# An expert's first product run by pairs of quarters: one change to a tuned attention and mixture-of-experts kernel

## The chip, the cores and the metric

The kernel runs on one core of one Trainium2 chip. The metric is device time in microseconds, the median of several executions: 2615.45 us for the kernel before (three runs, 2614.93 to 2617.84). One further execution was recorded by the hardware profiler; it took 2614.48 us, and its span from the first to the last instruction is 2612.6 us. All rows below are from that execution.

## The reference, cut to what matters

Three stages run one after the other on 3072 tokens of width 512, all in float32.

```python
x = chunked_attention(q, k, v, mem_k, mem_v)          # 4 x 8 heads, 768 tokens, head width 64
h = x @ w_in; x = (h * clip(h + 3, 0, 6) / 6) @ w_out # hidden width 2048
P = exp(x @ w_gate - max)                             # 3072 x 8
for _ in range(8): P = rows and columns of P normalised in turn (sinkhorn)
for e in range(8):
    h = maximum(x @ w1[e], 0)                         # 512 -> 1024
    out += P[:, e:e+1] * (h @ w2[e])                  # 1024 -> 512
```

## The kernel before, in words

Every large product is made of three TensorE passes on operands that are split into a high and a low part (`passes`, L192 to L196): high weight by high operand, high by low, low by high. ACT makes the high part (a copy with rounding, `split`, L178), DVE the low part (a subtraction, L183).

The first stage (attention) and the second (the dense layer) run together in a loop over `steps`: two passes over the hidden width, each over 8 tiles of 384 tokens and 8 slices f of the hidden width. One such f-step of pass two is 12 matmuls of the first kind and 12 of the second. The x tile of 384 tokens is spilled to DRAM in pass one and loaded again for pass two (`x_load`, L364; `x_split`, L368, one quarter kt at a time). Beside this a "factory" (L456) on GpSimd forms the sums of quarters of the expert weights w1 and w2 that the third stage needs and stores them in DRAM.

The third stage (L892 on) handles 3 token blocks of 1024 tokens; each block meets 8 experts, so there are NM = 24 pairs n of block and expert. Each product of an expert is done by a scheme with seven products in place of eight: weights and operands are seen as 2 x 2 quarters, seven combinations of weight quarters (A11, A12, A22 and the sums S1 to S4) meet seven operands (B11, B21, B22 and the sums T1 to T4). For the first product the operands of x (tiles `xo`) stay in SBUF for a whole token block; they are made by `x_ops` for the first block and half by half by `x_half_load` and `x_half` at the change of block. `FIRST` gives the order of the seven; k runs over four column tiles of the hidden half. `first_product(n, k, p)` is 2 x 3 = 6 matmuls of 512 columns into a PSUM tile. The terms of a quarter of h accumulate partly in PSUM: `first_out` copies partial sums into tiles `cp` (ACT, L648) for p 0 to 2, and for p 3 to 5 DVE adds a copy and the PSUM tile into a tile `g` (L657); for p 6 ACT applies relu directly (L655). In the next step `positive` applies relu in place (ACT, L663) and `gated` multiplies by the gate (GpSimd, L670). The weights w1 of one k come as one tile of 7 x 256 columns (`w1_load`, 384 KB and 512 KB), its high part is made by ACT (L567); its low part is made by DVE for the first token block (L576) and stored, and loaded from DRAM for the later blocks.

The second product takes h's tiles as operands: `make` forms the T sums of h in four parts (DVE L692, for the last expert half of it on GpSimd), the high parts `oh` (ACT L701) and low parts `ol` (DVE L706), and the high and low part of the w2 tile (L607, L613; the staging tile has one buffer, so the next load waits for it). `second_product(n, mi, q)` is again 6 matmuls; `second_out` adds its result to y (DVE L735).

What sets the order is written out by hand. `order` (L916) is a list of steps; a step holds a first product, a second product, or both. Each engine and SyncE's DMA queue run their instructions in the order in which this loop issues them, and wait in order. Before, 28 + LEAD = 33 first products come alone, then 5 second products alone, then pairs, and at the end 28 second products alone. `makes` puts the four parts of a second operand four steps ahead of its use. The sinkhorn iterations run as a generator between the steps (L947), on DVE, with small matmuls on TensorE; then `gates` writes the gates to DRAM and they are loaded, broadcast. `halves` (L936 to L940) puts the 14 halves of the next block's x operands into the steps after (n = last expert, k = 3, p = 0).

Of the kernel before, what the change touches and what calls it, by code (L numbers as in the profile page):

```python
# [1 line left out]

# [6 lines left out]
F32 = mybir.dt.float32  # L9
# [20 lines left out]
HB = 512  # L30
# [3 lines left out]
NG = 12  # L34
LEAD = 5
# [3 lines left out]
def attn_moe_moe(ctx: ExitStack, tc: tile.TileContext, qk, vw, wi, wo, wa, wb, wg, out):  # L39
# [41 lines left out]
    ws1 = [dr_p.tile([128, 2, 4, 256], F32, name=f"ws1{j}") for j in range(NP // 2)]  # L81
    ws2 = [dr_p.tile([128, 4, 4, 256], F32, name=f"ws2{e}") for e in range(NE)]
    wl1 = [dr_p.tile([128, 7, 256], F32, name=f"wl1{q}") for q in range(NP)]
# [309 lines left out]
    def sinkhorn():  # L393
# [12 lines left out]
        for _ in range(8):  # L406
# [36 lines left out]
    FIRST = ((A11, "B11", "a"), (S1, "T1", "c"), (S2, "T2", "a"), (A12, "B21", "b"), (S3, "T3", "a"),  # L443
             (S4, "B22", "c"), (A22, "T4", "a"))

# [5 lines left out]
            "T4": ("T2", "B21", "T2")}  # L451
    NM = NSB * NE
    xo = {}
    w1s, w1, w2s, w2, gq, op, yc = {}, {}, {}, {}, {}, {}, {}

    def factory():  # L456
# [8 lines left out]
        def of_w1(q):  # L465
# [11 lines left out]
            def store():  # L477
                nc.sync.dma_start(out=ws1[q // 2][:, q % 2], in_=t[1])
# [23 lines left out]
    def x_ops(sb, p, tag):  # L502
# [7 lines left out]
        for n in ("B11", "T1", "T2", "B21", "T3", "B22", "T4"):  # L510
# [30 lines left out]
    X_ORDER = ("B11", "T1", "T2", "B21", "T3", "B22", "T4")  # L541
# [15 lines left out]
    def w1_load(j):  # L557
        if j < NM * NF // 2:
            s = w1s[j] = w1s_p.tile([128, 7, 256], F32, tag="w1s", name="w1s")
            q = j % NP  # L560
            nc.sync.dma_start(out=s[:, :3], in_=wa[q].rearrange("p (a f) -> p a f", a=4)[:, 1:])
            nc.sync.dma_start(out=s[:, 3:], in_=ws1[q // 2][:, q % 2])

    def w1_hi(j):
        if j < NM * NF // 2:
            hi = w1_p_tile("h")
            nc.scalar.activation(out=hi, in_=w1s[j], func=AF.Copy)  # L567
            w1[j] = hi

    def w1_p_tile(t):  # L570
        return w1r_p.tile([128, 7, 256], F32R, tag=f"w1{t}", name=f"w1{t}", bufs=2)

    def w1_lo(j):
        if j < NP:
            lo = w1_p_tile("l")
            nc.vector.tensor_tensor(out=lo, in0=w1s.pop(j), in1=w1[j].bitcast(F32), op=ALU.subtract)  # L576
            w1[j] = w1[j], lo
        elif j < NM * NF // 2:
            w1[j] = w1[j], w1l.pop(j)

    def w1_lo_load(j):

        if NP <= j < NM * NF // 2:
            lo = w1l[j] = w1_p_tile("l")
            nc.sync.dma_start(out=lo.bitcast(F32), in_=wl1[j % NP])

    def w1_lo_store(j):
        if j < NP:
            nc.sync.dma_start(out=wl1[j], in_=w1[j][1].bitcast(F32))
# [460 lines left out]
```

## Time and profile before

| | |
|---|---|
| median of runs | 2615.45 us |
| profiled execution | 2614.48 us, span 2612.6 us, mean granted TensorE clock 0.988 |
| TensorE, VectorE, ScalarE, GpSimd busy | 98%, 69%, 53%, 38% |
| DMA | 543 MB, 208 GB/s mean |
| chain that ended last | TensorE 86%, VectorE 7%, DMA 3%, ScalarE 2% |

How to read it: PE is TensorE, PEld its weight loads, DVE is VectorE, ACT is ScalarE, POOL is GpSimd, SP is SyncE, whose queue issues the DMAs. In rows of instructions "out<-in" are the program's tile names and "x" a count; L is a line of the kernel. A wait row says who waited for whom: total us, times, longest. PEclk is the granted clock as a share of full speed.

### The profile page before, as it was taken

The page shows a single profiled execution, that of the slowest core. Times are in us where ns is not written, and L with a number is a line of the kernel's source. Part 1 is how long each engine was busy: PE and PEld are TensorE (multiplying, and loading weights), DVE is VectorE, ACT ScalarE, POOL GpSimd, SP SyncE. Part 2 cuts the span into 40 slices and gives each one's busy share as a digit, 9 for nine tenths or more (in the row PEclk, how much of TensorE's full clock was granted, in tenths as well). Part 3 has the DMA queues.
Part 4 walks back from the last instruction along what each step waited for, and adds up shares of the span by engine and source line. Part 5 has one row for each costly group of instructions (what it writes and reads, how often), then busy time and mean ns, then how long its engine had stood idle before and what let it go on. Part 6 is the DMA issues. An engine that isn't in the chain of part 4 may idle for free.

```text
span 2612.6 us, 34019 instructions
## 1 busy us (share of the span) xinstructions
PE 2550.9 (98%) x12621; PEld 2196.5 (84%) x12621; DVE 1812.7 (69%) x2115; ACT 1390.7 (53%) x2323; POOL 989.4 (38%) x693
## 2 busy tenths in 40 slices
PE   7999999999989999999989999999999999999998
PEld 7899999999968888888768888888878888888886
DVE  6767766557478999898875666666575566566666
ACT  6656654122255555555556555555565655555553
POOL 1035554454006535444432434433333334333332
PEclk9899999999999999999989999999999999999999
DMA  7468867775255666656656666665575655565643
GB/s 203 125 206 274 280 219 273 234 251 189 87 178 191 238 212 205 239 194 210 218 197 222 224 227 228 215 219 203 182 260 188 221 204 203 181 203 204 203 167 137
DMA packets 198102, 543.06 MB, mean 208 GB/s; under 512 B 18960, under 2 KB 80592, under 8 KB 197936
## 3 DMA queue, kind: packets, MB, share of 16 engines
q1 hardware_dynamic: 197936, 540.89, 61.4%
q8 instruction: 99, 1.62, 0.3%
q14 instruction: 67, 0.55, 0.1%
HBM read 414.89 MB, written 125.93 MB: 207 GB/s over the span
## 4 chain that ended last, share of the span: by engine, by line
PE 86%; DVE 7%; DMA 3%; ACT 2%; issue 1%; SPq 0%; POOL 0%; DVEq 0%; ACTq 0%
PE oa L195 6%; PE oa L196 6%; PE oa L194 6%; PE ga L195 6%; PE ga L196 6%; PE ga L194 6%; PE pa L194 3%; PE oc L195 3%; PE oc L196 3%; PE oc L194 3%; PE ph L194 3%; PE ph L195 3%; PE ph L196 3%; PE pa L196 3%; PE gc L194 3%; PE pa L195 3%
## 5 line engine op out<-in xcount | busy, mean ns | idle before, releaser
L670 POOL TENSOR_TENSOR g<-g,pb 128x512 f32<-128x512 f32 x368 | 676.7, 1855 | 1207.6 <-ACT g L663 1065.1
L701 ACT ACTIVATE oh<-g 128x1024 fp32r<-128x1024 f32 x336 | 355.3, 1058 | 540.2 <-PE oa L196 204.6
L706 DVE TENSOR_TENSOR ol<-g,oh 128x1024 fp32r<-128x1024 f32 x336 | 461.7, 1378 | 219.1 <-ACT oh L701 218.7
L692 DVE TENSOR_TENSOR g<-g 128x1024 f32<-128x1024 f32 x188 | 323.4, 1752 | 21.4 <-POOL g L670 21.4
L194 PE MATMUL ga<-xo,w1h 128*128 128x512 f32 x768 | 302.4, 394 | 9.0 <-DVE g L657 8.2
L195 PE MATMUL ga<-xo,w1h 128*128 128x512 f32 x768 | 300.7, 392 | 1.6 <-DVE xo L183 1.6
L195 PE MATMUL oa<-ol,w2h 128*128 128x512 f32 x768 | 300.1, 391 | 1.8 <-DVE ol L706 1.8
L194 PE MATMUL oa<-oh,w2h 128*128 128x512 f32 x768 | 300.4, 391 | 0.6 <-ACT oh L701 0.6
L196 PE MATMUL ga<-xo,w1l 128*128 128x512 f32 x768 | 300.2, 391 | 0.0
L196 PE MATMUL oa<-oh,w2l 128*128 128x512 f32 x768 | 299.9, 390 | 0.0
L607 ACT ACTIVATE w2h<-w2s 128x1024 fp32r<-128x1024 f32 x168 | 177.6, 1057 | 77.5 <-DMA w2s<-ws 29.5
L663 ACT ACTIVATE g<-g 128x512 f32<-128x512 f32 x288 | 174.9, 620 | 65.8 <-DVE g L657 65.7
L308 ACT ACTIVATE t<-ph,half 128x384 f32<-128x384 f32 x128 | 74.6, 582 | 223.6 <-PE ph L196 223.6
L463 POOL TENSOR_TENSOR fs<-fr 128x256 f32<-128x256 f32 x128 | 113.1, 883 | 205.5 <-DMA ws<-fs 196.9
L735 DVE TENSOR_TENSOR y<-y,oa 128x512 f32<-128x512 f32 x174 | 118.9, 683 | 97.9 <-PE oa L196 97.2
L194 PE MATMUL ph<-xh,wah 128*128 128x384 f32 x512 | 181.2, 354 | 1.0 <-ACT xh L178 1.0
L194 PEld LDWEIGHTS ga<-xo,w1h 128*128 128x128 f32 x768 | 145.1, 189 | 41.5 <-issue 5.5
L195 PE MATMUL ph<-xl,wah 128*128 128x384 f32 x512 | 175.7, 343 | 3.7 <-DVE xl L183 3.6
L196 PE MATMUL ph<-xh,wal 128*128 128x384 f32 x512 | 174.9, 342 | 0.0
L194 PE MATMUL pa<-hh,wbh 128*128 128x384 f32 x512 | 174.6, 341 | 0.0
L195 PEld LDWEIGHTS oa<-ol,w2h 128*128 128x128 f32 x768 | 144.9, 189 | 32.7 <-DVE ol L706 2.5
L195 PEld LDWEIGHTS ga<-xo,w1h 128*128 128x128 f32 x768 | 144.7, 188 | 32.6 <-DVE xo L183 3.5
(144 smaller groups left out, 5629.6 us busy)
## 6 DMA issues: line engine op xcount, KB each, us to landing
w1l<-wl SPq DMA_DIRECT2D x64, 896.0 KB, 7.2
w2l<-wl SPq DMA_DIRECT2D x112, 512.0 KB, 3.7
w1s<-ws SPq DMA_DIRECT2D x96, 512.0 KB, 4.8
w2s<-ws SPq DMA_DIRECT2D x96, 512.0 KB, 5.2
w1s<-in_wa_dram SPq DMA_DIRECT2D x96, 384.0 KB, 3.7
w2s<-in_wb_dram SPq DMA_DIRECT2D x144, 256.0 KB, 4.3
ws<-fs SPq DMA_DIRECT2D x64, 512.0 KB, 5.8
wl<-w1l SPq DMA_DIRECT2D x32, 896.0 KB, 7.4
```

The costliest lines, as they stand in the source:

```text
L194: nc.tensor.matmul(ps, wh, xh, start=start, stop=False, skip_group_check=more)
L195: nc.tensor.matmul(ps, wh, xl, start=False, stop=False, skip_group_check=more)
L196: nc.tensor.matmul(ps, wl, xh, start=False, stop=stop, skip_group_check=more)
L308: nc.scalar.activation(out=t, in_=ps, func=AF.Relu, scale=1.0 / 6.0, bias=half)
L463: nc.gpsimd.tensor_tensor(out=s[o], in0=a, in1=b, op=f)
L607: nc.scalar.activation(out=hi, in_=w2s[m], func=AF.Copy)
L663: nc.scalar.activation(out=g, in_=g, func=AF.Relu)
L670: nc.gpsimd.tensor_tensor(out=g, in0=g, in1=p, op=ALU.mult)
L692: eng.tensor_tensor(out=o, in0=gq[n, x, i], in1=gq[n, y, i], op=ALU.subtract)
L701: nc.scalar.activation(out=hi, in_=gq[n, b, i], func=AF.Copy)
L706: nc.vector.tensor_tensor(out=lo, in0=gq[n, b, i], in1=op[m, i].bitcast(F32), op=ALU.subtract)
L735: nc.vector.tensor_tensor(out=t, in0=t, in1=yo[c, dc], op=ALU.add)
```

## The change: what it does

The four k of a first product are taken in two pairs: for each pair and each p, both k in turn. A12 by B21 comes first, then A11 by B11; the partial sums are copied into the tiles of h themselves and completed there, so the tiles `cp` go, and h's tiles number 13 instead of 12. Per p and pair of k there is one small w1 tile of 2 x 256 columns, staged in three buffers and kept in seven; load, high part, low part and store are issued piece by piece, about six pieces ahead. The factory's w1 sums are laid out in DRAM to match. LEAD falls from 5 to 1, and no second products run alone before the pairs: 29 first products alone, then pairs, then 29 second products alone. The x operands are made in the new order, one half in each of 14 steps at a block change. The sinkhorn generator is advanced in two of three steps instead of four of seven, and the gates follow in it after a further yield. In pass one's last tile `x_load(0)` is issued at f = 1 instead of 3, and its four splits at f = 3 to 6 instead of 4 to 7.

```diff
-NG = 12
-LEAD = 5
+NG = 13
+LEAD = 1
-    ws1 = [dr_p.tile([128, 2, 4, 256], ...
+    ws1 = [dr_p.tile([128, 4, 2, 256], ...
-    wl1 = [dr_p.tile([128, 7, 256], F32, name=f"wl1{q}") for q in range(NP)]
+    wl1 = [dr_p.tile([128, 2, 256], F32, name=f"wl1{g}") for g in range(7 * NP // 2)]
-    FIRST = ((A11, "B11", "a"), (S1, "T1", "c"), (S2, "T2", "a"), (A12, "B21", "b"), (S3, "T3", "a"),
+    FIRST = ((A12, "B21", "b"), (A11, "B11", "a"), (S1, "T1", "c"), (S2, "T2", "a"), (S3, "T3", "a"),
              (S4, "B22", "c"), (A22, "T4", "a"))
+    FIRST_OUT = ("B11", "B11", "B22", "B12", "B22", "B12", "B21")
-        for n in ("B11", "T1", "T2", "B21", "T3", "B22", "T4"):
+        for n in X_ORDER:          # ("B21", "B11", "T1", "T2", "T3", "B22", "T4")
...
+    def w1_load(g):
+        if g < NW:
+            q, a = g // 7 % (NP // 2), FIRST[g % 7][0]
+            s = w1s[g] = w1s_p.tile([128, 2, 256], F32, tag="w1s", name="w1s", bufs=3)
+            if a < S1:
+                of = wa[2 * q:2 * q + 2].rearrange("k p (a f) -> p k a f", a=4)[:, :, a + 1]
+            else:
+                of = ws1[q][:, a - S1]
+            nc.sync.dma_start(out=s, in_=of)
+    def w1_hi(g):
+        if g < NW:
+            w1[g] = w1_p_tile("h")
+            nc.scalar.activation(out=w1[g], in_=w1s[g], func=AF.Copy)
+    def w1_lo(g):
+        if g < 7 * NP // 2:
+            lo = w1_p_tile("l")
+            nc.vector.tensor_tensor(out=lo, in0=w1s.pop(g), in1=w1[g].bitcast(F32), op=ALU.subtract)
...
     def first_product(n, k, p):
-        new = p in (0, 1, 3)
+        new = p < 3
-        wh, wl = w1[4 * n + k]
+        wh, wl = w1[7 * (2 * n + k // 2) + p]
...
     def first_out(n, k, p):
+        ps, b, i = ch[FIRST[p][2], k], FIRST_OUT[p], k // 2
+        if k % 2 == 0 and p in (0, 2, 3, 6):
+            gq[n, b, i] = g_p.tile([128, 2, HB], F32, tag="g", name="g", bufs=NG)
+        g = gq[n, b, i][:, k % 2]
+        if p in (0, 2, 3):
+            nc.scalar.activation(out=g, in_=ps, func=AF.Copy)
+        elif p == 6:
+            nc.scalar.activation(out=g, in_=ps, func=AF.Relu)
         else:
-            nc.vector.tensor_tensor(out=g, in0=cp[other], in1=ch[c], op=ALU.add)
+            nc.vector.tensor_tensor(out=g, in0=g, in1=ps, op=ALU.add)
...
-            if (pe, b) == (1, NB1 - 1):
-                for do, j in {2: ((w1_hi, 0),), 3: ((w1_lo, 0), (w1_load, 1)), 6: ((w1_hi, 1),),
-                              7: ((w1_lo, 1), (w1_load, 2))}.get(f, ()):
-                    do(j)
+            if (pe, b) == (1, NB1 - 1) and 1 <= f < 7:
+                w1_hi(f - 1)
+                w1_lo(f - 1)
+                if f < 6:
+                    w1_load(f + 2)
...
-                if f == 3:
+                if f == 1:
                     x_load(0)
...
-            if f >= 4 and n < NB1 and (pe or b == NB1 - 1):
-                x_split(n, f - 4)
+            r = f - (4 if pe else 3)
+            if 0 <= r < KT and n < NB1 and (pe or b == NB1 - 1):
+                x_split(n, r)
...
-        H = [(n, k, p) for n in range(NM) for k in range(4) for p in range(7)]
+        work = chain(sinkhorn(), gates())       # gates yields once after its copy
+        H = [(n, k + j, p) for n in range(NM) for k in (0, 2) for p in range(7) for j in range(2)]
-        order = [(H.pop(0), None) for _ in range(28 + LEAD)] + [(None, O.pop(0)) for _ in range(LEAD)]
+        order = [(H.pop(0), None) for _ in range(28 + LEAD)]
-        quarters = {3: "B11", 4: "B22", 5: "B12", 6: "B21"}
+        quarters = {1: "B11", 4: "B22", 5: "B12", 6: "B21"}
-                halves[base + 1 + r * 11 // 13] = halves.get(base + 1 + r * 11 // 13, []) + [(sb, r)]
+                halves[base + 1 + r] = [(sb, r)]
-            if work and i % 7 in (0, 1, 2, 6) and next(work, 0) == 0:
+            if work and i % 3 != 1 and next(work, 0) == 0:
...
+                g = 7 * (2 * n + k // 2) + p
+                if k % 2:
+                    w1_load(g + 8)
+                    w1_lo_load(g + 6)
+                    w1_hi(g + 6)
+                else:
+                    if g:
+                        w1_lo(g + 5)
+                    for m in range(4 if g == 0 else 0):
+                        w1_lo_store(m)
+                    w1_lo_store(g + 4)
```

## Rows read from the trace of the kernel before

**Rows 1.** The page's busy times: TensorE, us, share of the span, instructions.

```profile
PE 2550.9 (98%) x12621; PEld 2196.5 (84%) x12621; DVE 1812.7 (69%) x2115; ACT 1390.7 (53%) x2323; POOL 989.4 (38%) x693
```

**Rows 2.** Busy us (instructions) of each engine in eight stretches, clock, DMA share.

```profile
core 0: us, PE busy (x) PEld busy (x) DVE busy (x) ACT busy (x) POOL busy (x), PEclk, DMA share, GB/s
718.00:772.00 54.00, 49.95 (x224) 39.51 (x224) 39.08 (x96) 27.59 (x42) 0.00 (x0) 1.00 0.43 153
772.00:792.00 20.00, 14.77 (x59) 11.56 (x58) 15.20 (x13) 8.94 (x12) 3.37 (x2) 0.91 0.79 252
860.00:1240.00 380.00, 379.51 (x1673) 313.71 (x1672) 346.93 (x296) 211.40 (x264) 180.15 (x87) 1.00 0.64 216
1300.00:1365.00 65.00, 54.57 (x214) 42.38 (x213) 48.77 (x51) 35.55 (x48) 19.48 (x12) 0.89 0.54 184
1950.00:2015.00 65.00, 61.12 (x256) 48.90 (x255) 40.32 (x42) 34.45 (x44) 20.71 (x12) 0.95 0.55 195
2560.00:2580.00 20.00, 16.15 (x60) 11.99 (x60) 15.90 (x11) 7.44 (x8) 13.51 (x6) 0.91 0.42 139
430.00:440.00 10.00, 6.80 (x31) 6.23 (x30) 7.57 (x10) 3.71 (x7) 7.09 (x8) 0.83 0.77 258
440.00:450.00 10.00, 10.00 (x60) 10.00 (x59) 6.08 (x9) 4.61 (x9) 3.78 (x5) 1.00 0.83 281
```

**Rows 3.** TensorE's waits from 1280 to 1345 us: total us, times, longest.

```profile
PE ga L194 <- DVE g L657: 5.4, 2, 3.5
PE gc L194 <- ACT xo L178: 3.3, 1, 3.3
```

**Rows 4.** ScalarE's wait for loads of x halves, same stretch.

```profile
ACT xo L178 <- DMA xs<-x2d: 8.2, 2, 5.0
```

**Rows 5.** TensorE's longest wait from 760 to 860 us.

```profile
PE oc L194 <- ACT oh L701: 3.7, 1, 3.7
```

**Rows 6.** ScalarE's wait for the load of w2, 755 to 870 us.

```profile
ACT w2h L607 <- DMA w2s<-ws: 10.9, 3, 5.2
```

**Rows 7.** TensorE's waits from 380 to 450 us.

```profile
PE ph L195 <- DVE xl L183: 2.2, 1, 2.2
PE ph L194 <- ACT xh L178: 1.0, 1, 1.0
```

**Rows 8.** Timeline at the end: start us, duration us, engine, line, instruction.

```profile
2560.89 2.39 POOL L692 TENSOR_TENSOR g<-g 128x1024 f32<-128x1024 f32 x1
```

**Rows 9.** VectorE groups by line, 720 to 772 us: busy us, mean ns, idle before.

```profile
L576 DVE TENSOR_TENSOR w1l<-w1s,w1h 128x1792 fp32r<-128x1792 f32 x3 | 6.1, 2020 | 0.0
L657 DVE TENSOR_TENSOR g<-cp,gb 128x512 f32<-128x512 f32 x5 | 3.4, 686 | 0.5 <-PE gb L196 0.4
```

**Rows 10.** Groups of the x operands' halves, whole span.

```profile
L183 DVE TENSOR_TENSOR xo<-xs,xo 128x512 fp32r<-128x512 f32 x28 | 23.6, 852 | 18.1 <-ACT xo L178 18.1
L178 ACT ACTIVATE xo<-xs 128x512 fp32r<-128x512 f32 x28 | 17.2, 622 | 16.2 <-DMA xs<-x2d 11.2 <-DMA xs<-xt 5.0
```

**Rows 11.** Timeline of pass one's end: a subtraction of 512 columns with GpSimd at work.

```profile
409.72 1.22 DVE L183 TENSOR_TENSOR wal<-sa,wah 128x512 fp32r<-128x512 f32 x1
```

**Rows 12.** VectorE groups by line, 860 to 1240 us.

```profile
L706 DVE TENSOR_TENSOR ol<-g,oh 128x1024 fp32r<-128x1024 f32 x71 | 106.5, 1510 | 10.0 <-ACT oh L701 10.0
L692 DVE TENSOR_TENSOR g<-g 128x1024 f32<-128x1024 f32 x40 | 68.5, 1746 | 3.6 <-POOL g L670 3.6
L613 DVE TENSOR_TENSOR w2l<-w2s,w2h 128x1024 fp32r<-128x1024 f32 x35 | 54.9, 1569 | 7.9 <-ACT w2h L607 7.8
L576 DVE TENSOR_TENSOR w1l<-w1s,w1h 128x1792 fp32r<-128x1792 f32 x20 | 47.2, 2359 | 0.0
```

**Rows 13.** DMA issues of the page: count, KB each, median us to landing.

```profile
w2s<-ws SPq DMA_DIRECT2D x96, 512.0 KB, 5.2
w2s<-in_wb_dram SPq DMA_DIRECT2D x144, 256.0 KB, 4.3
xs<-x2d SPq DMA_DIRECT2D x36, 256.0 KB, 6.2
```

More of the change, by code (lines that the diff above doesn't have):

```diff
@@ L1 @@
 from contextlib import ExitStack
+from itertools import chain
 import concourse.bass as bass
@@ L80, in attn_moe_moe @@
     xp = [dr_p.tile([128, KT, B1], F32, name=f"xp{b}") for b in range(NB1)]
-    ws1 = [dr_p.tile([128, 2, 4, 256], F32, name=f"ws1{j}") for j in range(NP // 2)]
+    ws1 = [dr_p.tile([128, 4, 2, 256], F32, name=f"ws1{j}") for j in range(NP // 2)]
     ws2 = [dr_p.tile([128, 4, 4, 256], F32, name=f"ws2{e}") for e in range(NE)]
-    wl1 = [dr_p.tile([128, 7, 256], F32, name=f"wl1{q}") for q in range(NP)]
+    wl1 = [dr_p.tile([128, 2, 256], F32, name=f"wl1{g}") for g in range(7 * NP // 2)]
     wl2 = [dr_p.tile([128, 4, 256], F32, name=f"wl2{m}") for m in range(7 * NE)]
@@ L587, in w1_lo_store @@
-    def w1_lo_store(j):
-        if j < NP:
-            nc.sync.dma_start(out=wl1[j], in_=w1[j][1].bitcast(F32))
+    def w1_p_tile(t):
+        return w1r_p.tile([128, 2, 256], F32R, tag=f"w1{t}", name=f"w1{t}", bufs=7)
+    def w1_load(g):
[7 more added lines that the diff above has]
+            nc.sync.dma_start(out=s, in_=of)
@@ new lines, in w1_hi, with w1_lo_load @@
+    def w1_hi(g):
[4 more added lines that the diff above has]
+        if g < 7 * NP // 2:
+            lo = w1_p_tile("l")
+            nc.vector.tensor_tensor(out=lo, in0=w1s.pop(g), in1=w1[g].bitcast(F32), op=ALU.subtract)
+            w1[g] = w1[g], lo
+        elif g < NW:
+            w1[g] = w1[g], w1l.pop(g)
+    def w1_lo_load(g):
+        if 7 * NP // 2 <= g < NW:
+            lo = w1l[g] = w1_p_tile("l")
+            nc.sync.dma_start(out=lo.bitcast(F32), in_=wl1[g % (7 * NP // 2)])
@@ L591, in attn_moe_moe, with w1_lo_store @@
+    def w1_lo_store(g):
+        if g < 7 * NP // 2:
+            nc.sync.dma_start(out=wl1[g], in_=w1[g][1].bitcast(F32))
     w1l, w2l = {}, {}
@@ L892, in attn_moe_moe @@
         ps_g, ps_o = (ctx.enter_context(pool(n, 1, PSUM)) for n in ("ps_g", "ps_o"))
-        w2r_p, g_p, op_p, y_p, pb_p, tmp_p, out_p = (
-            ctx.enter_context(pool(n, 1)) for n in ("w2r", "g", "op", "y", "pb", "tmp", "out"))
-        work = sinkhorn()
-        next(work)
+        w2r_p, g_p, op_p, y_p, pb_p, out_p = (
+            ctx.enter_context(pool(n, 1)) for n in ("w2r", "g", "op", "y", "pb", "out"))
         def bank():
```

65 lines of the change are left out of this document (11 added, 54 removed).

## The prediction

> **What bounds the kernel now.** I read the page's busy shares first: TensorE is busy 98% of the span [rows 1]. Its matmul work stays the same (672 first and 672 second products, six matmuls each), so the change can win or lose only TensorE time that is not steady running. The steady rate comes from the table of stretches, 860 to 1240 us: 1673 matmuls in 380 us at clock 1.00, 0.227 us each; a product takes 1.36 us, a step with a first and a second product 2.72 [rows 2]. In the table's other stretches TensorE falls behind this rate, and the matmul counts give what each costs, clock included:
> - a, 430 to 440, start of pass two: 31 matmuls where the next 10 us hold 60: 29 x 0.167 = 4.8 us.
> - b1, 718 to 772, start of the expert part: 33 first products are 198 matmuls, 45.0 us of 54; 9.0 us go to the small sinkhorn matmuls and to waits.
> - b2, 772 to 792, the five unpaired second products and after: 59 where 88 would fit, 6.6 us.
> - c, 1300 to 1365, change of x operands to the second token block: 214 of 286, 16.4 us. The granted clock is 0.89: after the stops TensorE runs for a while at the lower of its levels (1.2 of 2.4 GHz), which the count includes.
> - d, 1950 to 2015, the same for the third block: 256 of 286, 6.8 us.
> - e, 2560 to 2580, the unpaired end: 60 of 88, 6.4 us.
>
> Together 50 us. Then the waits, for what ended last in each. In c TensorE waits for DVE's adds (L657) and for new x operands (L178) [rows 3], and ACT in turn for the loads of x halves [rows 4]. In b it waits for ACT's high part of the second operand [rows 5], behind an ACT that waited up to 5.2 us for the w2 load [rows 6]. In a it waits for the last quarter of the x tile [rows 7]. At e the half of T1 that POOL forms starts only at 2560.89 [rows 8].
>
> **a: x tile sooner.** The load is issued two f-steps earlier, the four splits one f-step earlier; an f-step of pass two is 24 matmuls, 24 x 0.167 = 4.0 us. The late split was waited for 1.0 + 2.2 us [rows 7], less than 4.0, so the wait goes; next on DVE are that step's weight splits, needed steps later. On SP the load passes two steps' weight loads and delays them by one 768 KB transfer at most; they too are needed a step or more later. Gain 4 (0 to 4.8).
>
> **b: start of the expert part.** Now 29 first products run alone, then pairs. The second weight tile gets the time of four pairs, 10.9 us, instead of four lone products, 5.4, so ACT's 5.2 us wait for w2 is covered and most of b2 goes. But DVE gets tight. In the 54 us it was busy 39.1 [rows 2], 6.1 of that three low parts of w1 of 2.02 each [rows 9]. Now it has 13 small low parts. A subtract of 128x512 is not in this stretch; the x operand's row is 0.852 with POOL beside it [rows 10], the 1792-wide one in proportion 0.58; I take 0.69, the adds of this width here [rows 9]: 9.0 us. DVE then needs 39.1 - 6.1 + 9.0, less two adds (1.4) = 40.6 us, TensorE 29 x 1.36 + some 5 of sinkhorn = 44.4: 91% instead of 72%, in a loop where the two take turns. I allow 2 us more waiting in b1, and 1.5 us before the first second product, whose low part stands at the end of DVE's queue. Gain 6.6 - 2 - 1.5 = 3 (at worst 1.22 a piece, as a 128x512 subtract took beside POOL [rows 11]: 7 more, so -4; at best b2 and a third of b1's 9.0 gone: 10).
>
> **c and d: new x operands.** Before, operands came free one step apart, 14 halves were spread over 12 steps, and the new expert wanted the first after 7: a slack of six steps that fell to one. In pairs an operand comes free every two steps, its two halves are split in the next two, and it is wanted eleven steps (30 us) later: the waits on xo go. So do the waits on L657: an accumulator that DVE reads is written again four steps later instead of two; only the third term (an ACT copy) is reused after two. What is late next is the low part of the second product, made two steps ahead of its reader. DVE's work per four steps in the first change: with a T sum 3.49 + 1.57 + 3.02 (two sums, w2 low, two ol) [rows 12] + two y adds and 1.7 first-product adds at 0.69, 2.5 = 10.6; without one 7.1; mean 8.85; plus four x halves of 0.852 [rows 10] = 12.3 in 10.9 us. It falls 1.4 us behind in four steps, 5 us in fourteen, about what two steps (5.4) cover; with the clock I leave 3.4 us. c: gain 13 (8 if half the loss stays with the loads, 16.4 if nothing is left). d: DVE is busy 40 of 65 us [rows 2], so 6 of 6.8 (3 to 6.8).
>
> **e: the end.** The last quarters used to be complete four to one first products before the next second product, B12 two; now B12 is complete four before, and its multiplies on POOL are through sooner, so T1's half there starts some 3 us earlier against TensorE. The chain of sum, oh and ol repeats for T2 at the pace of lone products, so not all goes: 4 of 6.4 (0 to 6.4).
>
> **Small pieces in the first token block.** Per expert four w1 low parts of 2.359 us become 14 of 0.852: 11.9 instead of 9.4 [rows 10, 12]. DVE is busy 346.9 of 380 us, so of an expert's 76.3 us (336 matmuls) 6.6 are free, then 4.1. TensorE lost nothing there (379.5 of 380 [rows 2]); I take +2 us for seven experts; 0 at 0.69 a piece, 8 at 1.22 (17.1, 1.1 beyond the free time, times seven). ACT is busy 211.4 of 380 us; its 14 pieces at 0.622 [rows 10] are 8.7 per expert in place of the same elements in four: nothing. Partial sums in h's tiles: the copy goes to another tile, the add has the same shape: nothing. SP issues 28 instead of 12 w1 transfers per expert, each waiting only for work a step or two old; a 256 KB transfer in runs of 1 KB lands in 4.3 us [rows 13] and is issued four steps (10.9 us, alone 5.4) ahead: nothing, and in the lone part a few tenths, within b.
> The Trainium skill (Perfetto Trace Analysis, DMA Optimizations) speaks against splitting: transfers under 2 KB carry a significant cost each, and batching helps. By it, w1's 7.3 MB per expert, of the 16.5 that 216 GB/s move in 76 us, would at double price take the DMA share from 0.64 to 0.92 [rows 2], and x halves would land late again: the first rival, at its time. The rows do not bear it out: 256 KB in 1 KB runs lands in 4.3 us, 512 KB in 4 KB runs in 5.2 [rows 13].
>
> **Sum.** -4 -3 -13 -6 -4 +2 = -28 against the profiled execution's 2614.5 (span 2612.6 and 1.9 around it): 2586.5; the median of the runs is 1.0 higher, so 2587.
>
> **Rivals.**
> 1. The x halves stay late. Three buffers rotate; 6.2 us to land [rows 13] plus 0.62 and 0.85 for the split make 7.7 for three halves against three steps, 8.2; each us more in landing puts the last of 14 halves 14/3 us later, in ACT's queue ahead of all else. For: ACT stood up to 5.0 us at such loads [rows 4]. Against: eleven steps of slack. Then half of c and d stays: 28 - 11 = 17 gained, 2598.
> 2. Nothing is left at all places: 4.8 + 10 + 16.4 + 6.8 + 6.4 = 44: 2571. For: TensorE's own queue has room everywhere; against: the 12.3 in 10.9.
> 3. Slower: in the first token block groups with a T sum run over DVE's time. With small pieces one takes 10.6 + 14 x 0.852 / 7 = 12.3 us against 10.9, a group without 8.8. If that slack cannot be banked, because low parts wait for ACT's high parts, each of 32 groups costs 1.4 us: 45 us, less the 30 gained elsewhere: 2630. It decides from 30/32 = 0.94 us per group. Against: by the same count it was 12.0 before (2.359 x 4 / 7 in place of 1.7), and TensorE ran through.
> 4. The handovers hang on something else than operand order, and the lost time returns as other waits: 2614.
>
> **Chances.** Forecast (2576 to 2596) 0.60, rival 1 0.15, rival 2 0.12, rival 3 0.08, rival 4 0.05. Faster by over 0.2% (5.2 us, about what can be told from no change here): 0.60 + 0.15 + 0.12 = 0.87; same 0.05; slower 0.08. The range runs from rival 2 with 4 us more to rival 1 with 6 less: 2567 to 2604; outside lie rivals 3 and 4 and a few points of the tails.
>
> **What would show it.** TensorE's waits for xo and for L657's add gone around 1290 and 1940, with clock 1.00; no wait at the first matmuls of pass two; one short wait at the first oa, longer ones at L418; 860 to 1240 still near 380 busy with DVE near 94%. Wrong would be: under 375 there, ACT waits for xs of 10 us and more with TensorE standing, or b1 losing over 15 us.

## The result: 41 us faster, where 28 were forecast

The changed kernel takes 2574.23 us (median of 4 runs, 2570.0 to 2574.82), the kernel before 2615.19 us (median of 4, 2612.24 to 2617.84). The ratio is 0.984, with a 95% interval from 0.9823 to 0.9857. The forecast was 2587 with a range from 2567 to 2604, so the time lies inside; it is close to the second rival's 2571, in which nothing is left of the lost time at any place.

The page after: TensorE's busy time, to be held against [rows 1].

```profile
PE 2531.7 (99%) x12621; PEld 2186.3 (85%) x12621; DVE 1787.1 (70%) x2195; ACT 1399.4 (54%) x2563; POOL 933.8 (36%) x693
```

The number of matmuls is the same. VectorE (DVE) has 80 instructions more and is busy 25.6 us less. The table of stretches after, with the columns of [rows 2]; the stretches are those of [rows 2], moved to where the same work now stands:

```profile
709.00:754.00 45.00, 43.91 (x201) 35.38 (x201) 37.42 (x104) 25.96 (x48) 0.00 (x0) 1.00 0.62 191
754.00:774.00 20.00, 19.79 (x87) 16.06 (x86) 16.91 (x17) 13.11 (x21) 2.59 (x2) 1.00 0.85 281
774.00:860.00 86.00, 84.47 (x371) 69.31 (x370) 82.93 (x70) 50.93 (x76) 54.04 (x27) 1.00 0.64 213
860.00:1240.00 380.00, 380.00 (x1678) 314.64 (x1677) 349.30 (x348) 215.65 (x315) 161.25 (x87) 1.00 0.64 214
1230.00:1300.00 70.00, 68.89 (x302) 56.14 (x301) 60.85 (x66) 44.64 (x68) 23.84 (x14) 1.00 0.74 248
1885.00:1950.00 65.00, 65.00 (x288) 53.82 (x287) 50.66 (x54) 42.20 (x64) 24.85 (x15) 1.00 0.72 237
...
2515.00:2535.00 20.00, 16.84 (x72) 13.03 (x72) 16.86 (x14) 9.24 (x11) 13.31 (x5) 1.00 0.49 158
...
425.00:435.00 10.00, 10.00 (x60) 10.00 (x59) 9.34 (x13) 6.67 (x14) 7.30 (x8) 1.00 0.86 282
```

Read them by the matmul counts, as the prediction did. The start of pass two holds 60 in 10 us where it held 31. The 20 us after the lone part hold 87 where they held 59. The change to the second token block holds 302 in 70 us (308 would be steady) where 214 stood for 286, and the granted clock there is 1.00 instead of 0.89. The change to the third block holds 288, the full rate. Only the end still stops: 72 of 88, a loss of 3.6 us instead of 6.4.

A part of each stop was the clock that followed it. By the PEclk of [rows 2], 10 x 0.17 + 20 x 0.09 + 65 x 0.11 + 65 x 0.05 + 20 x 0.09 = 15.7 of the 50 us that the prediction counted were lost to the lower level of the clock (1.2 GHz) after TensorE had stood; the same stretches are at 1.00 now.

TensorE's waits in the changed kernel (engine, tile and line that waits, what it waits for, total us, times, longest), first from 700 to 860 us, which answers to [rows 5]:

```profile
PE oa L196 <- DVE ol L706: 0.8, 1, 0.8
PE oc L196 <- DVE ol L706: 0.7, 1, 0.7
PE sk L910 <- DVE pe L905: 0.7, 1, 0.7
...
PE sk L419 <- DVE cs L416: 0.4, 1, 0.4
...
```

Then from 860 to 2460 us, which holds both block changes and so answers to [rows 3]; this is the whole list:

```profile
PE oa L196 <- DVE ol L706: 1.1, 2, 0.8
```

The waits for new x operands and for L657's add are gone. No wait at all is shown from 380 to 450 us, where [rows 7] had 3.2.

To say where each microsecond went I measured landmarks in both traces: the first matmul of the first product (E0), the first of the second product, and the first output transposes of each token block, which end a block's 672 steps.

| stretch, us | before | after | gained | forecast |
|---|---|---|---|---|
| first stage, up to the last attention score | 376.2 | 372.4 | 3.8 | not in the change |
| from there to E0 (holds a) | 342.8 | 336.7 | 6.1 | a: 4 |
| E0 to the first block's output (holds b, c and the small pieces) | 672.5 | 649.9 | 22.6 | b, c, pieces: 3 + 13 - 2 = 14 |
| first to second block's output (holds d) | 621.0 | 613.0 | 8.0 | d: 6 |
| second to third block's output (holds e) | 585.6 | 581.7 | 3.9 | e: 4 |

They add up to the 44.4 us between the two spans. 3.8 of them lie ahead of the change and are not its work (the last section). The landmarks also hide a shift: with the pairs one step ahead, one more first product, 1.36 us, is done before a block's output, so that much work moved from the last line into the third. For the same work the third line gained 24.0 us and the last 2.5. Inside the third line, b and c separate by counts. From E0 to the first second product 33 lone first products took 52.9 us, 8.0 over their 1.36 us each; now 30 take 45.6, 4.8 over. So b1 gained 3.2 and b2 6.4 (6.6 lost before, 0.2 now): b is 9.6. c lost 16.4 and now loses (308 - 302) x 0.227 = 1.4: 15.0. From 774 to 860 us the changed kernel loses 1.8 that were not lost before (371 matmuls where 379 would fit; the two waits for `ol` above stand there, at 843 and 855 us), and 860 to 1240 us holds 5 matmuls more, 1.1. Together 23.9 for the 24.0 found.

### The profile page after: what moved, and what is told of

Its sections match the earlier page's. It is cut to its first block, busy times and chain, and to the rows that moved or that the text cites. A ratio compares the mean times of both kernels' runs of the same rounds, so it can differ in the third digit from the quotient of the medians.

```text
span 2568.2 us, 34838 instructions
## 1 busy us (share of the span) xinstructions
PE 2531.7 (99%) x12621; PEld 2186.3 (85%) x12621; DVE 1787.1 (70%) x2195; ACT 1399.4 (54%) x2563; POOL 933.8 (36%) x693
## 4 chain that ended last, share of the span: by engine, by line
PE 91%; DVE 5%; DMA 1%; ACT 1%; issue 1%; SPq 0%; POOL 0%; DVEq 0%; ACTq 0%
PE oa L196 6%; PE oa L197 6%; PE oa L195 6%; PE ga L195 6%; PE ga L197 6%; PE ga L196 6%; PE pa L195 3%; PE ph L195 3%; PE gc L195 3%; PE gc L197 3%; PE oc L197 3%; PE gc L196 3%; PE oc L195 3%; PE oc L196 3%; PE pa L197 3%; PE pa L196 3%
## 5 line engine op out<-in xcount | busy, mean ns | idle before, releaser
L670 POOL TENSOR_TENSOR g<-g,pb 128x512 f32<-128x512 f32 x368 | 614.5, 1687 | 1220.0 <-ACT g L663 821.7
L706 DVE TENSOR_TENSOR ol<-g,oh 128x1024 fp32r<-128x1024 f32 x336 | 434.6, 1296 | 234.2 <-ACT oh L701 233.6
L692 DVE TENSOR_TENSOR g<-g 128x1024 f32<-128x1024 f32 x188 | 291.8, 1590 | 0.0
L576 ACT ACTIVATE w1h<-w1s 128x512 fp32r<-128x512 f32 x336 | 208.6, 621 | 2.0 <-DMA w1s<-in_wa_dram 2.0
L612 ACT ACTIVATE w2h<-w2s 128x1024 fp32r<-128x1024 f32 x168 | 177.2, 1055 | 45.4 <-DMA w2s<-in_wb_dram 18.7
L663 ACT ACTIVATE g<-g 128x512 f32<-128x512 f32 x288 | 177.4, 616 | 25.5 <-DVE g L657 25.5
L197 PE MATMUL pa<-hh,wbl 128*128 128x384 f32 x512 | 171.5, 335 | 0.0
```

The costliest lines, as they stand in the source:

```text
L197: nc.tensor.matmul(ps, wl, xh, start=False, stop=stop, skip_group_check=more)
L576: nc.scalar.activation(out=w1[g], in_=w1s[g], func=AF.Copy)
L612: nc.scalar.activation(out=hi, in_=w2s[m], func=AF.Copy)
L663: nc.scalar.activation(out=g, in_=g, func=AF.Relu)
L670: nc.gpsimd.tensor_tensor(out=g, in0=g, in1=p, op=ALU.mult)
L692: eng.tensor_tensor(out=o, in0=gq[n, x, i], in1=gq[n, y, i], op=ALU.subtract)
```

## Experiments

Each is a small edit of the kernel before or of the changed kernel, and every ratio is against the kernel before. "Block 1" and so on are the stretches of the table above. The theory was the prediction's: operand order ends the stops of c and d through its eleven steps of slack, the x tile those of a, pairs those of b2.

**x_sooner**, the kernel before with the two edits of pass two alone:

```diff
-                if f == 3:
+                if f == 1:
                     x_load(0)
...
-            if f >= 4 and n < NB1 and (pe or b == NB1 - 1):
-                x_split(n, f - 4)
+            r = f - (4 if pe else 3)
+            if 0 <= r < KT and n < NB1 and (pe or b == NB1 - 1):
+                x_split(n, r)
```

> The kernel before with the earlier load and split of pass two's first x tile alone. Theory (the last quarter of the x tile is what TensorE waits for): the stretch at the start of pass two holds 60 matmuls in 10 us instead of 31, and the kernel is 4.8 us faster, about 2610.5. Rival (the weight splits queued on DVE beside it are late as well): the stop stays, under 2 us gained.

Measured: 2611.65 us (2607.5 to 2612.95, 11 runs), ratio 0.9985 (0.9976 to 0.9993). Its row of the table from 420 to 450 us:

```profile
420.00:450.00 30.00, 30.00 (x175) 30.00 (x174) 23.81 (x33) 13.52 (x27) 17.94 (x19) 1.00 0.80 263
```

TensorE runs through at clock 1.00, and the stretch to E0 falls from 342.8 to 338.0 us: 4.8, the whole stop. Term a is shown.

**no_x_halves**, the kernel before without any x operands for the later blocks; they are computed with the first block's x.

```diff
-            for sb, r in halves.get(i, ()):
+            for sb, r in ():
```

> The kernel before without the reload and split of x operands at the two changes of token block (later blocks are computed with the first block's x). Theory (the stops at the handovers come from those halves, the waits on DVE's adds included, since the halves hold up both queues): all 286 matmuls per 65 us at 1300 and 1950, 23 us faster, about 2592. Rival (an accumulator that DVE reads is written again too soon, whatever x does): waits on L657 stay and 8 to 15 us of the 23 with them, about 2602.

Measured: 2589.04 us (2588.35 to 2591.94), ratio 0.9897 (0.9882 to 0.9912). Its rows for the two block changes:

```profile
1300.00:1365.00 65.00, 65.00 (x289) 53.84 (x288) 48.45 (x49) 37.05 (x46) 23.07 (x14) 1.00 0.65 218
1950.00:2015.00 65.00, 65.00 (x305) 53.95 (x303) 40.40 (x40) 40.08 (x53) 19.53 (x12) 1.00 0.63 211
```

Nothing is lost in either, and the waits on L657's adds are gone with the halves, though accumulators and order are as before. Block 1 falls by 16.9 us and block 2 by 8.0, to 613.0, which is the changed kernel's value. So making the halves causes the stops of c and d. Whether the new operand order is what ended them, this run does not tell.

**halves_late**, the changed kernel with eight of the eleven steps of slack taken away.

```diff
-                halves[base + 1 + r] = [(sb, r)]
+                halves[base + 9 + r] = [(sb, r)]
-                halves.setdefault(base - 4 + r, []).append((sb, r - 2))
+                halves.setdefault(base + 4 + r, []).append((sb, r - 2))
```

> The changed kernel with the 14 x halves loaded and split eight steps later, so that an operand is ready three steps before its use instead of eleven. Theory (slack of the operands is what the pairs bought at the block changes): waits of TensorE on xo return and 5 to 12 us are lost, 2580 to 2586. Rival (what mattered is one half per step and the four steps between a read and the next write of an accumulator; slack beyond three steps is not used): under 2 us.

Measured: 2573.89 us (2571.01 to 2575.2), ratio 0.9838 (0.9815 to 0.9861): nothing is lost. The stretch that held 302 matmuls in the changed kernel:

```profile
1230.00:1300.00 70.00, 70.00 (x311) 57.96 (x310) 60.51 (x63) 41.41 (x62) 23.41 (x14) 1.00 0.67 227
```

It is now full, and block 1 is 2.0 us shorter. Three steps of slack do as well as eleven, so the eleven steps that the prediction put its weight on were not what was needed.

**halves_squeezed**, the halves later still and two in a step, which leaves the first operand one step of slack and each later one a step more.

```diff
-                halves[base + 1 + r] = [(sb, r)]
+                halves.setdefault(base + 12 + r // 2, []).append((sb, r))
-                halves.setdefault(base - 4 + r, []).append((sb, r - 2))
+                halves.setdefault(base + 7 + r, []).append((sb, r - 2))
```

> The changed kernel with the 14 x halves in seven consecutive steps, two per step, just ahead of their use, so that they come faster than three buffers can be loaded. Theory (before, a block change cost time because the halves stood in ACT's and DVE's queues waiting for loads, and all other work of these queues stood behind them): the stops at 1300 and 1950 come back, 10 us or more in all, with ACT waiting over 10 us for xs. Rival (the large w1 operations in the same queues, or the distance between a read and the next write of an accumulator, made the stops): under 3 us.

Measured: 2587.92 us (2586.8 to 2591.88), ratio 0.9897 (0.9882 to 0.9912); block 1 is 7.5 us longer than in the changed kernel, block 2 9.2. TensorE's waits from 1240 to 1340 us, the whole list:

```profile
PE gb L195 <- ACT xo L179: 2.7, 1, 2.7
PE ga L195 <- ACT g L653: 2.0, 1, 2.0
```

ScalarE (ACT) at the loads of x, 1220 to 1340 us:

```profile
ACT xo L179 <- DMA xs<-xt: 2.7, 3, 1.5
ACT xo L179 <- DMA xs<-x2d: 1.4, 2, 0.7
```

Some two thirds of the loss of c and d are back (16.7 of 24.9), with the same two kinds of wait as [rows 3]: an x operand, and an accumulator that another engine still holds. The theory wanted ACT to wait over 10 us at loads, and that came only in sum: 4.1 us in this change and 6.8 in the second. But the changed kernel stands 8.7 us at them in the first change alone (shown under c and d) and loses 1.4. So splits packed close to their readers cost the time, and the loads are not the main part of it. Which counts for more, two splits in a step or the short slack, this kernel can't tell. It keeps the pairs and the small w1 pieces and stops all the same, so neither ends the stops without room for the halves; the pairs were not run without the small pieces.

**lone_seconds**, the changed kernel with the start of the kernel before: five first products more alone, then five second products alone. From there the pairs run with no lead, as before.

```diff
-        order = [(H.pop(0), None) for _ in range(28 + LEAD)]
+        order = [(H.pop(0), None) for _ in range(33)] + [(None, O.pop(0)) for _ in range(5)]
```

> The changed kernel with the old beginning: 33 first products alone, then five second products alone, then pairs. Theory (b2 is ACT waiting for the single staging buffer of w2 while lone second products run at 1.36 us): a wait of 3 to 4 us at the first oc returns and the kernel loses 6 us, about 2580. Rival (the stop came from DVE's lag behind sinkhorn and the large w1 parts): within 2 us of 2574.

Measured: 2588.52 us (2585.93 to 2590.89), ratio 0.9896 (0.9882 to 0.991), 14 us over the changed kernel. TensorE's waits from 710 to 800 us:

```profile
PE oc L195 <- ACT oh L701: 2.1, 1, 2.1
PE oc L196 <- DVE ol L706: 1.7, 1, 1.7
...
```

and from 1270 to 1330 us, the whole list:

```profile
PE oa L195 <- ACT xo L179: 2.9, 1, 2.9
PE oa L196 <- DVE ol L706: 0.8, 1, 0.8
```

The stop of b2 is back (some 5 us) with the wait of [rows 5]. Some 5 are lost at the change of operands, where ACT again stands at x loads, and the last block takes 585.6 us, just what it took before. I had not expected the last two. What of the 3.9 us at the end is the lead's own stands under e below.

**old_pace**, the changed kernel with the old pace of the sinkhorn steps.

```diff
-            if work and i % 3 != 1 and next(work, 0) == 0:
+            if work and i % 7 in (0, 1, 2, 6) and next(work, 0) == 0:
```

> The changed kernel with sinkhorn advanced in four of seven steps as before, so that the gates come three steps later. Theory (even spacing leaves DVE two steps between its column sums and the matmul that reads them, and that is why TensorE hardly waited in the lone part): waits at the sinkhorn matmuls come back to 1.5 us or more and the lone part is 2 to 3 us longer. Rival (pairs and small pieces did it): under 1 us.

Measured: 2579.06 us (2578.62 to 2579.79), ratio 0.986 (0.9847 to 0.9874). The lone part takes 45.4 us against 45.6, but that is not the same work: 17 of the 21 small sinkhorn matmuls lie in it instead of all, and the last four come among the pairs. So this run does not show what the pace is worth. The median is 4.8 us higher, though the two intervals overlap. In the traces 2.6 us of it lie in block 1, all after the lone part, where those four matmuls now stand (how much of it is theirs is not shown), and 1.6 in the last block, which is a fall of the clock (shown under e).

**order_alone**, the kernel before with the short lead, no lone second products and the new pace, but its own tiles and quarters.

```diff
-LEAD = 5
+LEAD = 1
-        order = [(H.pop(0), None) for _ in range(28 + LEAD)] + [(None, O.pop(0)) for _ in range(LEAD)]
+        order = [(H.pop(0), None) for _ in range(28 + LEAD)]
-            if work and i % 7 in (0, 1, 2, 6) and next(work, 0) == 0:
+            if work and i % 3 != 1 and next(work, 0) == 0:
```

> The kernel before with the new beginning alone: 29 first products, then pairs, sinkhorn in two of three steps; no pairs of quarters, no small pieces, x as before. Theory (b is a matter of order and pace): b1 and b2 give 8 to 9.6 us, and e 1 to 3, about 2605. Rival (the large w1 parts of 2.02 us in DVE's queue are what made TensorE wait): 3 us or less.

Measured: 2612.96 us (2607.0 to 2616.98, 10 runs), ratio 0.9988 (0.9976 to 1.0). The waits of TensorE from 710 to 790 us:

```profile
PE sk L908 <- DVE pe L904: 3.1, 1, 3.1
...
PE ga L194 <- DVE g L657: 2.2, 2, 1.1
...
```

30 lone products take 52.2 us here against 45.6 in the changed kernel, and 3.1 of that is one wait of the gates' first transpose for DVE's copy. 52.2 us are 11.3 over their 1.36 each, where the 33 of the kernel before were 8.0 over: with the old tiles the new beginning makes b1 3.3 us longer. The next 20 us hold 79 matmuls where 59 stood, so most of b2 goes; c stays (238 matmuls of 308 from 1290 to 1360 us). The whole gain is far from the 10 us expected, and the interval of the ratio reaches 1.0. The last block falls to 582.9 us with the lead alone, without pairs and with the quarters in the old order.

**order_and_yield**, that kernel with the gates' work handed out through the generator, with a pause after its copy as in the change.

```diff
-                gates()
-                gate_load(0)
-                gate_load(1)
...
+        work = chain(sinkhorn(), gates())    # gates yields once after its copy, loads at its end
```

> The kernel before with the new beginning, and the gates following in the sinkhorn generator after a yield, as in the change; k one by one and large w1 tiles as before. With the beginning alone the lone part took 52.2 us to the first oa, 45.6 in the changed kernel, the same 30 first products. Theory (the transposes that waited 3.1 us for the copy in the same step are the largest single part): about 49.5 us. Rival (DVE is late there in any case, and the wait moves to the next product): 51 us or more.

Measured: 2606.47 us (2601.49 to 2608.43), ratio 0.996 (0.9946 to 0.9974). The lone part is 49.3 us where 49.5 were expected: the pause is worth 2.9. The wait of the transpose fell by half of that; the rest is in no wait that the trace names. The waits for L657's adds (L658 here) stay. From 718 to 769 us:

```profile
PE ga L195 <- DVE g L658: 2.2, 2, 1.1
PE sk L908 <- DVE pe L903: 1.6, 1, 1.6
...
```

**order_yield_split**, that one with each low part of w1 in smaller pieces, the second half of them and the next w1 load one step later.

```diff
...
                     if p == 4:
-                        w1_lo(4 * n + k + 1)
-                        w1_load(4 * n + k + 2)
+                        w1_lo(4 * n + k + 1, 0)      # columns 1 to 3 of 7
+                    if p == 5:
+                        w1_lo(4 * n + k + 1, 1)      # columns 4 to 6, and 0
+                        w1_load(4 * n + k + 2)
```

> As the run with the new beginning and the yield, but each large low part of w1 (2.02 us) is formed in two steps by three instructions of 768, 768 and 256 columns, and the next load follows one step later. Theory (what makes TensorE wait in the lone part is the longest stretch that DVE is not at the sinkhorn chain): the lone part is another 1.5 to 3 us shorter, near 47. Rival (DVE's total counts, or ACT's 1.7 us high part that stands before the copy a product needs): no shorter, or longer by the extra instructions.

Measured: 2629.17 us (2625.08 to 2636.15), ratio 1.0055 (1.0036 to 1.0073). The lone part is 47.7 us, 1.6 shorter. From 721 to 770 us the transpose waits less and the adds (L663 here) as long as without the edit:

```profile
PE ga L195 <- DVE g L663: 2.2, 2, 1.1
PE sk L913 <- DVE pe L908: 0.7, 1, 0.7
...
```

But block 1 is 27.3 us longer than without the edit, spread over 790 to 1270 us. The row of the table for 860 to 1240 us:

```profile
860.00:1240.00 380.00, 369.60 (x1606) 301.19 (x1606) 344.24 (x322) 202.76 (x254) 149.78 (x83) 1.00 0.61 207
```

What ACT waits for in the same stretch, and then what SyncE's queue waits for:

```profile
...
ACT w2h L613 <- DMA w2s<-ws: 29.3, 6, 6.1
ACT w2h L613 <- DMA w2s<-in_wb_dram: 27.7, 9, 5.3
...
```

```profile
SPq L562 <- DVE w1l L581: 142.1, 19, 13.2
...
```

DVE's groups there: the low part of w2 (busy us, mean ns, then idle just before it).

```profile
L619 DVE TENSOR_TENSOR w2l<-w2s,w2h 128x1024 fp32r<-128x1024 f32 x34 | 48.0, 1412 | 28.1 <-ACT w2h L613 28.1
```

DVE is not over its time: 344.24 us busy, less than the 346.93 of [rows 2], and it stands idle 28.1 us for the high part of w2, where [rows 12] has 7.8. ACT waits 57.0 us for the w2 loads, 25.2 without the edit (order_and_yield, the same stretch, where TensorE does 1677 matmuls). SyncE's queue, which also issues those loads, stands up to 13.2 us at a w1 load whose buffer a low part on DVE still holds, and 142.1 in all; without the edit it is up to 6.9 and 94.8 in all. I read it so from these rows: a load that waits at the head of this queue made others late. The moved load and the smaller pieces were not run apart.

**low_parts_twice**, the changed kernel with every low part of w1 in the first token block computed twice into the same tile.

```diff
+            nc.vector.tensor_tensor(out=lo, in0=w1s[g], in1=w1[g].bitcast(F32), op=ALU.subtract)
             nc.vector.tensor_tensor(out=lo, in0=w1s.pop(g), in1=w1[g].bitcast(F32), op=ALU.subtract)
```

> The changed kernel with every small low part of w1 in the first token block formed twice, the same subtraction into the same tile. DVE had 6.1 us free of 75.9 per expert (349.3 busy in 380); 14 more pieces of 1.13 us are 15.8, 9.7 too many. Theory (DVE's idle time can be used whole): 9.7 x 8 = 78 us slower at most, about 2650, DVE near 100% from 780 to 1300. Rival (DVE's pieces are long only because POOL works beside them, so the surplus is the uncontended 0.69 a piece, 9.7 - 6.1 = 3.6 per expert): about 29 us, 2603. If the idle time could not be used at all, 15.8 x 8 = 126 us, 2700.

Measured: 2617.96 us (2613.45 to 2622.14, 10 runs), ratio 1.0007 (0.9995 to 1.0019). Its rows for the lone part and for the first block:

```profile
714.00:767.00 53.00, 46.58 (x203) 35.17 (x204) 45.68 (x117) 26.64 (x49) 0.00 (x0) 1.00 0.54 165
860.00:1240.00 380.00, 367.51 (x1585) 296.56 (x1584) 377.68 (x395) 203.61 (x298) 131.71 (x81) 1.00 0.62 204
```

In the block DVE is busy 377.68 of 380 us while TensorE falls behind (1585 matmuls where 1678 stood), and block 1 is 40.3 us longer, 7.4 of them in the lone part. The other 32.9 are near the rival's 29 and far from the 78, though the pieces took 0.97 and 1.04 us and not the 0.69 that the rival reckoned with. DVE's idle time in the block can be used almost whole. The lone part grows from 45.6 to 53.0 us: 13 more pieces at the 0.69 assumed are 9 us, and they cost 7.4, though DVE is busy only 45.68 of 53 us there. In that part the two engines take turns, and the added work on DVE was hardly hidden.

**tail_on_dve**, the changed kernel with the sums of the last second product all on DVE.

```diff
-                    eng = nc.gpsimd if n == NM - 1 and i else nc.vector
+                    eng = nc.vector
```

> The changed kernel with all T sums of the last expert on DVE instead of half of them on GpSimd. In the end part DVE's sum of 1.22 us took 3.04 while GpSimd's ran beside it for 3.3. Theory (the two slow each other and T2 waits for both): the 3.6 us lost there shrink to 1.5, 2 us faster. Rival (DVE is the longer queue: two sums, two low parts and two adds are 6.2 us in 5.4): 1 to 2 us slower.

Measured: 2572.45 us (2571.81 to 2574.21), ratio 0.9835 (0.9813 to 0.9858). The last block falls from 581.7 to 579.5 us, the 2 expected; by the whole time it is not told from the changed kernel, since the intervals overlap. In the changed kernel the two engines work on halves at the same time (timeline of POOL and of DVE: start, us, engine, line):

```profile
2518.08 3.38 POOL L692 TENSOR_TENSOR g<-g 128x1024 f32<-128x1024 f32 x1
2523.89 5.72 POOL L692 TENSOR_TENSOR g<-g 128x1024 f32<-128x1024 f32 x2 [2.42 <-DVE ol L706]
...
2524.32 3.04 DVE L692 TENSOR_TENSOR g<-g 128x1024 f32<-128x1024 f32 x1
```

In this kernel DVE does two halves one after the other:

```profile
2522.33 2.86 DVE L692 TENSOR_TENSOR g<-g 128x1024 f32<-128x1024 f32 x2
```

One half on DVE beside POOL (3.04 us) took longer than two on DVE without POOL's sum (2.86), and POOL's own take 2.4 to 3.4 each: here sharing the sum gains nothing.

**late_and_dve_tail**, the changed kernel with the edits of halves_late and of tail_on_dve, as the likely best version.

> The changed kernel with both edits that the traces of single runs favour: the x halves eight steps later (block one 2.0 us shorter from its first product to its first output transpose) and all T sums of the last expert on DVE (last block 2.2 us shorter). Theory (the two places do not touch): 4 us faster than the changed kernel, about 2570. Rival (both are chance of a single execution): within 1 us of 2574.

Measured: 2571.53 us (2566.9 to 2573.24), ratio 0.9829 (0.9814 to 0.9843). Block 1 (648.9 us) and the last block (579.5) are shorter by 1.0 and 2.2, but the interval overlaps the changed kernel's, so by the whole time it is not told from it.

## Why the prediction came out as it did, step by step

**What bounds the kernel: right.** All the gain behind the first stage is TensorE's time outside steady running, and 860 to 1240 us stayed full. The waits ended by the engines that the rows named.

**a: right.** 4 forecast; 4.8 in x_sooner, by the cause given. Nothing is late next.

**b: the step that was mis-sized**, 3 forecast and 9.6 measured, half of the 13 us by which the forecast missed. The failing step is "I allow 2 us more waiting in b1": a busy share of 91% was taken to cost 2 us. In the trace DVE is busy 37.42 of 45 us, 83% (the forecast had 40.6 of 44.4), and b1 loses 3.2 less than before, not 2 more. The loss that was feared did come with the old tiles: in order_alone b1 lost 3.3 more. Between its 52.2 us and the 45.6 of the changed kernel 2.9 is the pause in the gates' work and 1.6 the smaller low parts, which no longer hold DVE for 2.02 us each [rows 9] (in a run that moved a load as well). 2.1 is left, about the 2.2 us of waits for L657's adds that both runs with the old tiles show and the changed kernel does not. So the prediction counted the small pieces as work, rightly (13 took 0.674 us each), but it did not price the pause, and it reckoned with the accumulators that pairs leave free for longer only at c and d. The longer waits that it expected at L418 (now L419) are 0.4 us. For the 1.5 us before the first second product no wait is recorded; the two for `ol` come some 90 us later. What b2 lost did go as reasoned, and lone_seconds brings it back.

**c and d: right in size and in kind, wrong in one reason.** 13 and 6 forecast, some 15 and 8.0 measured. no_x_halves shows that the halves cause the stops, and that 16.9 and 8.0 were to be had. The eleven steps of slack were far more than needed: three do; one, growing to seven, with two splits in a step does not. That it was the order by pairs, and not the small pieces beside it, that made the room is argued and was not run apart. And the lead, which the prediction treated only at the start, takes part: without it some 5 us are lost again at c. The count of DVE's work (12.3 us in 10.9) was too dark, since the low parts of the second product were waited for only 1.1 us in all from 860 to 2460. ACT's waits at x loads in the kernel before were those of [rows 4] and, in the same stretch, these:

```profile
ACT xo L178 <- DMA xs<-xt: 5.0, 1, 5.0
```

In the changed kernel, from 1220 to 1310 us:

```profile
ACT xo L179 <- DMA xs<-xt: 5.9, 4, 2.6
ACT xo L179 <- DMA xs<-x2d: 2.8, 1, 2.8
```

ACT still stands 8.7 us at them, where it stood 13.2. That the list of TensorE's waits holds none for xo shows that the same wait can be free: what counts is who stands behind it.

**e: right in size by luck.** 4 forecast, 3.9 in the table, but that number is made of three things. 1.4 is the first product that the lead moved ahead of the landmark. Most of the rest is the clock. Here are 46 us from shortly before the last first product, in the kernel before, in x_sooner (whose edit acts 2000 us earlier), in the changed kernel and in old_pace (whose edit acts before 770 us):

```profile
2552.00:2598.00 46.00, 42.15 (x176) 33.53 (x175) 36.03 (x33) 21.01 (x22) 16.75 (x7) 0.96 0.38 127
2549.80:2595.80 46.00, 42.16 (x185) 33.74 (x184) 36.68 (x33) 21.61 (x23) 16.79 (x7) 1.00 0.39 126
2508.80:2554.80 46.00, 42.84 (x189) 34.60 (x188) 34.29 (x32) 21.44 (x23) 16.79 (x8) 1.00 0.43 141
2517.00:2563.00 46.00, 42.86 (x180) 34.51 (x179) 33.26 (x31) 21.13 (x22) 16.79 (x8) 0.96 0.44 141
```

With the old end as with the new one the clock falls to the lower level in some executions after a stop and in others not, and the last block is 1.6 us longer or shorter by it: 585.6 and 584.0 with the old end, 583.3 and 581.7 with the new. At the same clock the change is worth 2.3 us in the last block, and 0.9 when the shifted product is taken off: that is the third thing. The reason given was that B12 is complete sooner, so POOL begins its half of T1 sooner. But lone_seconds keeps the new quarters and gains nothing (585.6 us), and order_alone has the old quarters and the lead and falls to 582.9, at the same 0.96. So what little was gained is the lead's. POOL's half begins 5.3 us after the start of the last first matmul (2518.08, shown above, and 2512.8), where it began 4.9 after it (2560.89 in [rows 8], and 2556.0); with its reader one product of 1.36 us later by the lead, that is 1.0 sooner, not the 3 forecast, and it takes 3.38 us instead of 2.39. What is left to gain there is in good part the half on POOL (tail_on_dve, 2.2).

**Small pieces in the first block: 2 forecast, nothing measured.** DVE's groups after, 860 to 1240 us, against [rows 12]:

```profile
L706 DVE TENSOR_TENSOR ol<-g,oh 128x1024 fp32r<-128x1024 f32 x70 | 91.7, 1316 | 26.3 <-ACT oh L701 26.2
L581 DVE TENSOR_TENSOR w1l<-w1s,w1h 128x512 fp32r<-128x512 f32 x71 | 80.3, 1130 | 0.0
L692 DVE TENSOR_TENSOR g<-g 128x1024 f32<-128x1024 f32 x40 | 60.8, 1559 | 0.0
L618 DVE TENSOR_TENSOR w2l<-w2s,w2h 128x1024 fp32r<-128x1024 f32 x36 | 51.0, 1418 | 1.6 <-ACT w2h L612 1.5
```

A piece took 1.130 us, worse than the 0.852 assumed and near the bound of 1.22; 71 of them are 80.3 us where the large ones were 47.2. By the prediction's count 14 of them, 15.8 us, would have taken all the time that an expert leaves free (9.4 + 6.6). But the other groups became shorter (1.510 to 1.316, 1.746 to 1.559, 1.569 to 1.418), and DVE's whole grew by 2.4 us only. I read this as a slowing beside POOL that went from some instructions to others. DVE is at 92% (94% forecast), and low_parts_twice shows that the 30.7 us left can be used almost whole.

**The rivals.** Rival 1 (x halves stay late by the loads) did not come true, and even in halves_squeezed the loads are not the main cause. Of the DMA rows that answer to [rows 13],

```profile
w1s<-ws SPq DMA_DIRECT2D x192, 256.0 KB, 5.1
w2s<-ws SPq DMA_DIRECT2D x96, 512.0 KB, 4.7
...
w1s<-in_wa_dram SPq DMA_DIRECT2D x144, 256.0 KB, 4.8
w2s<-in_wb_dram SPq DMA_DIRECT2D x144, 256.0 KB, 5.4
xs<-x2d SPq DMA_DIRECT2D x36, 256.0 KB, 5.8
```

one became slower by 1.1 us and two sooner by about 0.5. Pieces of w1 in runs of 1 KB (from `in_wa_dram`) landed in 4.8 us, those of the same size in runs of 2 KB (from `ws`) in 5.1. The Trainium skill (Perfetto Trace Analysis, DMA Optimizations) counts transfers under 2 KB as costly. It gives no price; the double price was the prediction's own, and the prediction put it on all of w1. By the kernel's tiles only six of an expert's 28 w1 transfers go in runs of 1 KB, 1.6 of the 16.5 MB, and the others in 2 KB. At double price that gives an estimate of 0.64 x (1 + 1.6 / 16.5) = 0.70 for the DMA share of the first block, not 0.92. It stayed at 0.64, so no such cost shows here, but the rule was tested less hard than the prediction says. Rival 2 is nearly what happened: some 40 of its 44 went at the five places. Rival 3 (DVE over its time in the first block) would have needed more DVE work than the 30.7 us that were still free in these 380. Rival 4 falls by the time measured: what was lost at the block changes did not come back as other waits.

## What to carry to other kernels

Count the matmuls of a stretch against the steady rate, and give each stop its own term; the terms whose cover was named held to 2 us (e among them by luck), while a flat allowance for "tight" was off by 5. Look at the granted clock before a microsecond is put down to an edit: 1.6 of the 3.9 at the end came and went with it in kernels whose end is the same. Do not turn a busy share into a loss: here an engine at 83% with shorter instructions and a pause delayed its partner less than one at 72% with long ones, and an added load (low_parts_twice) told how much room was left. Before moving a load in an in-order queue, look for what is behind it, and check a suspected cause by giving each half of the edit alone: what the end of this kernel gained by the edit came from the lead, not from the order that was meant to do it.

## What the runs showed of the hardware that was not expected

The first stage, which no edit touches, differs from one execution to the next. From 65 to 130 us the traces hold 373 to 379 matmuls at a granted clock of 0.85 to 0.87 in nine of the kernels, and 386 to 413 at 0.89 to 0.95 in the other five; the attention ends between 372.4 and 378.4 us. The profile of the changed kernel is one of the quicker kind (413, 0.95) and that of the kernel before one of the slower (377, 0.86), which is the 3.8 us of the first line of the table. It may also be much of the 4 us between runs of one kernel; no kernel has two traces to show it.

How long one DVE instruction took beside POOL was no fixed price. The same 128x512 subtraction took 0.852 us on average [rows 10] and 1.130 in another place; without POOL, in the lone part, it took 0.674. Where pieces were added the larger instructions became shorter, which may mean that it depends on what else stands beside POOL; that was not run apart.
